# From step 1 on SyncE issues every copy within the chip, and the plan is re-timed for it

## The chip, the cores and the metric

The kernel runs on 1 core of one Trainium2 chip. The metric is the device time of one execution in microseconds (us). Where a per cent is given it is of the time before, 480.99 us.

## The reference

For 4 batches and 8 heads a gated linear attention runs over 768 tokens; its output is the input of a two-layer block with a piecewise gate:

```python
f = 1.0 / (1.0 + np.exp(-f_logit))
for t in range(S):                       # S = 768, D = 48
    state = f[:, :, t, :, None] * state + np.einsum('bhd,bhe->bhde', k[:, :, t], v[:, :, t])
    y[:, :, t] = np.einsum('bhd,bhde->bhe', q[:, :, t], state)
...
h = x @ w_in                             # x: 3072 x 384, w_in: 384 x 2048
g = np.where(h >= 1, h, np.where(h <= -1, 0.0, (h + 1) ** 2 / 4.0))
return g @ w_out                         # w_out: 2048 x 384
```

## The kernel before

**Steps and units.** The 768 tokens are cut into 6 steps of 128 tokens. Each step has 4 pairs of heads (the numbers n = 0 to 23 in the tables are 4 times the step plus the pair). Its attention result fills three tiles x (one row of tile per feature, 512 columns: 4 batches of 128 tokens), and on these the two-layer block runs in 16 units, one for each 128 of the 2048 middle features, so 96 units in all, numbered u = 0 to 95. `unit_1(u)` is nine matmuls of 128x512 into a bank `ph` (line 259); ScalarE (lines 262, 265), VectorE (270), ScalarE (273, giving `ghi`) and VectorE (276, giving `glo`) then make the two parts of the gate; `unit_2(u)` is nine matmuls from these into the three banks `po` (line 283). TensorE runs unit_1(u), then unit_2(u-1): between a unit's two halves lie the second half of the unit before it and the first half of the one after. Around step 1's end two units are cut in halves and paired differently; that is not touched here.

**Groups.** The attention of later steps is strewn between the units as groups of small matmuls. For a pair of numbers n, n+1 there are four kinds: the transposes of keys (`TURNS`: on TensorE for step 1, as stream transposes, line 735, on VectorE from step 2), the scores (line 702, then masks on line 708), the state parts (line 850, sums on lines 854 and 863; `begin` with them, line 757), and the outputs (line 789 and 757), after which lines 740 and 741 round the result into x. `VISITS` names for each n the unit after whose first half the scores, the state parts and the outputs stand.

**Copies within the chip.** The fourth pair of heads has no tile of its own in the block: its rows (16 of them at a time) are put into the spare rows of the other tiles. Hence two kinds of copies by DMA, both issued by `move` on line 301: `kq<-kq` gathers keys and queries of the fourth pair (6 pieces per step, line 584), and `x<-y` spreads its result over the three x tiles (6 pieces per step or half step, line 814). The six x pieces have to land before unit_1 of the next step's first unit. Every second piece goes by ScalarE's queue, the others by SyncE's. All other transfers (line 296: f, kq and v of the steps, raw weights, results) are issued by SyncE.

**Order.** A planner (`Plan.order`) lists the operations by engine: it walks through time with a cost for each operation (table `COST`, ns) and takes on each engine the operation that is due first. TensorE's own order is that of the program text. An engine executes its list in order, so an instruction that waits holds up whatever stands behind it; this holds for the DMA issues in ScalarE's list too. The DMAs share 8 semaphores in turn (`DMAHW0` to `DMAHW7` in the built program): an issue waits until the transfer that used its semaphore 8 transfers earlier has landed. Where the plan has a gap on TensorE in the first 20 us it puts matmuls on zeros there (line 337).

**Weights.** The weights come as 8-byte floats, 512 KB a piece into three buffers `raw` (25 pieces, used in the first 80 us); ScalarE (line 390), VectorE (392), ScalarE (396: the high part) and VectorE (397: the low part) split each. Later all pieces are loaded once more and searched for values out of range (line 407).

Of the kernel before, what the change touches and what calls it, by code (L numbers as in the profile page):

```python
# [10 lines left out]
F32 = mybir.dt.float32  # L11
# [14 lines left out]
NP = H // 2  # L26
# [15 lines left out]
NT = 3  # L42

SLICE = (1, 2, 0)
# [6 lines left out]

HOP, LANDING, PER_KB, NEAR, ADDING = 200, 2000, 3.0, 3500, 1500
LATENCY = dict(PE=235, ACT=140, DVE=110, POOL=150)
COST = dict(mm=227, narrow=120, scores=1100, scores_half=550, heads=950, thirds=1110, both=1090, begin=480, before=930, part=560, states=850, parts=830, turn=350, first=110, last=95,
            rows=316, turned_rows=150, scan=1140, dve=602, small=200, sums=467, gate=600, act=575, bits=660, round=485, copy=520, turned=412, sig=538, decay=226,
            issue=480, near=600, least=300)


TURNS = {4: 5, 5: 6, 6: 10, 7: 10, 8: 16, 9: 16, 10: 24, 11: 24, 12: 31, 13: 31, 14: 37, 15: 37, 16: 44, 17: 44, 18: 53, 19: 53, 20: 61, 21: 61, 22: 70, 23: 70}
VISITS = {4: (6, 7, 8), 6: (10, 11, 13), 8: (18, 22, 24), 10: (24, 28, 29), 12: (31, 35, 37), 14: (37, 43, 44), 16: (44, 48, 53), 18: (53, 57, 61), 20: (61, 67, 70), 22: (70, 72, 77)}  # L60
START = (("scores", 0), ("mask", 0, 0), ("mask", 0, 1), ("last", 0), ("scores", 1), ("mask", 1, 0), ("mask", 1, 1), ("last", 1),
         ("scores", 2, 0), ("last", 2, 0), ("scores", 2, 1), ("last", 2, 1), ("first", 0), ("first", 1),
         ("mask", 2, 1), ("mask", 3, 1), ("mask", 2, 0), ("mask", 3, 0), ("second", 0), ("second", 1), ("second", 2), ("second", 3))
# [17 lines left out]
class Plan:  # L81
# [7 lines left out]
    def add(self, engine, cost, emit, *deps, kb=0, near=0):  # L89
# [9 lines left out]
        spread(list(deps))  # L99
        cost, kind = COST[cost] if isinstance(cost, str) else cost, cost  # L100
        if engine == "PE":
# [67 lines left out]
def gla_moe(ctx: ExitStack, tc: tile.TileContext, ff, kqd, f0, vv, vad, vbd, wd, fixedd, gates, values, headsd, out):  # L169
    nc = tc.nc  # L170
# [12 lines left out]
    kq = tiles(NP, [128, 2 * N + B], F32, "kq")  # L183
# [12 lines left out]
    y3 = const.tile([R, 2, N], F32R, name="y3")  # L196
# [25 lines left out]
    def whole(t):  # L222
        return t[:, 2 * N:]
# [73 lines left out]

    def move(k, dst, src, *deps, near=NEAR):

        e, q = (("SP", nc.sync), ("ACT", nc.scalar))[k % 2]  # L300
        return add(e, "near", lambda: q.dma_start(dst, src), *deps, near=near)

    def vec(cost, fn, *deps):
# [15 lines left out]
    set_kq = add("POOL", 1500, lambda: nc.gpsimd.memset(kq[NP - 1], 0.0))  # L319
# [110 lines left out]
    turn = {"n": 0}  # L430
# [11 lines left out]
    state_of, moved, x_of, unit_in, unit_out = {}, {}, {}, {}, {}  # L442
# [106 lines left out]
    def elementwise(n):  # L549

        i, p = pairs[n]
        c = att[n] = {}
        k = n // 2 % 2
        by_half = i == HALVES
        h = p // 2 if by_half else None
        mine = ((0, 1), (2, 3))[p % 2] if by_half else (p,)
        ours = range(NT * i, NT * i + NT) if p == NP - 1 and not by_half else [NT * i + q for q in mine if q < NT]
        for m in ours:
            if by_half:
                gate(m, (h,))  # L560
            elif gates_of[m] is None:
                gate(m)
        before = [old(j, "y", "st") for j in (range(n - 2 * NP + NP - p, n - p) if i == HALVES + 1 else (n - 4,))]
        if by_half:
            k = p % 2
            if h == 0:
                c["lv"] = dma(v[k], vv[i, k], 384, before, att[2]["st"])
            else:
                c["lv"] = att[n - 2]["lv"]
        elif n % 2:  # L570
            c["lv"] = att[n - 1]["lv"]
        elif i == 0:
            c["lv"] = dma(va if p == 0 else vb, vad if p == 0 else vbd, 512 if p == 0 else 768)
        else:
            c["lv"] = dma(v[k], vv[i, p // 2], 384, before, att[2]["st"], moved[HALVES, 1])
        if NP - 1 in mine:

            every = range(NT * i, NT * i + NT)
            cols = slice(HW * h, HW * h + HW) if by_half else slice(0, 2 * N + B) if i else slice(0, N)
            gone = [old(NP * i - j, "sc", "y", "tr", "db") for j in ((1, 2, 3, 4) if i == HALVES + 1 else (1,))]  # L580
            for t, m in enumerate(every):
                o = gates_of[m]
                d = [o[a][h] for a in ("km", "qm", "pf")] if by_half else [o["km"], o["qm"], o["pf"][0]] if i else o["km"]
                to = [move(k, kq[NP - 1][z + 16 * SLICE[t]:z + 16 * SLICE[t] + 16, cols], kq[t][r:r + 16, cols], d, set_kq, gone, near=NEAR) for k, (r, z) in enumerate(((48, 0), (112, 64)))]
                o["to"] = o.get("to", []) + to
                c.setdefault("to", []).extend(to)
        if by_half:
            c["kq"] = [[gates_of[NT * i + q][a][h] for a in ("km", "qm")] for q in mine if q < NT] + c.get("to", [])
        else:
            c["kq"] = c["to"] if p == NP - 1 else [gates_of[m][a] for m in ours for a in ("km", "qm")]  # L590
        c["db"] = []
        for e, q in enumerate(mine if i > 0 else ()):
            nb = B // len(mine)
            at = n % 2 * B * D + e * nb * D
            bs = slice(0, B) if h is None else slice(h * nb, h * nb + nb)
            pf = whole(kq[q]) if h is None else kq[q][:, HW * h + 2 * HN:HW * (h + 1)]
            d = c["to"] if q == NP - 1 else gates_of[NT * i + q]["pf"][0 if h is None else h]

            def decayed(at=at, q=q, bs=bs, pf=pf):
                for j, b in enumerate(range(bs.start, bs.stop)):  # L600
                    nc.scalar.activation(ds[:, at + j * D:at + (j + 1) * D], state[:, q * B + b], AF.Copy, scale=pf[:R, j:j + 1])  # L601

            c["db"].append(sca(nb * COST["decay"], decayed, d, state_of[i - 1, q // 2], old(n - 2, "y", "se"), set_ds))
# [171 lines left out]
    def outputs(n):  # L775

        i, p = pairs[n]
        c, d = att[n], att[n + 1]
        held, where = c["to_y"]
        half_of = p // 2 if i == HALVES else None  # L780

        def emit():
            for k, before in ((1, later), (0, ds)):
                for m in range(B):
                    for e, h in TILES:
                        g, at = where[m][e]
                        (r, z), (pr, b) = HEADS[h], blocks(g)[at]
                        a = (g % 2 * B + at) * D
                        nc.tensor.matmul(held[h][1][64 * e:64 * e + D, m, T * k:T * k + T], before[r:z, a:a + D], query(g, pr, b)[r:z, T * k:T * k + T],  # L789
                                         start=False, stop=False)  # L790

        c["ys"] = add("PE", "before", emit, c["db"], d["db"], c["later"], c["yb"])
        y = c["y"] = d["y"] = add("PE", "part", attended(n, False), c["ys"])
        xt = x[i % 2]
        free = unit_in.get((i - 2, NJ - 1))

        def third(t):
            return [moved.get((i - 1, k)) for k in (None, 0, 1)] + c["se"] if t == NT else [free]

        if half_of is None:  # L800
            for t, (b, ps, _) in zip((p, p + 1), held):
                hi, lo = (y3[:, 0], y3[:, 1]) if t == NT else (xt[:, t, 0], xt[:, t, 1])
                x_of[i, t] = rounded(b, wide(ps)[:R], hi[:R], lo[:R], y, third(t))
            cs = ALL
        else:
            cs = cols_of(half_of)
            (b0, ps, _), (b1, qs, _) = held
            x_of[i, 0] = x_of[i, 2] = rounded(b0, wide(ps)[:R].rearrange("r (t n) -> r t n", t=2), xt[:R, 0:3:2, 0, cs], xt[:R, 0:3:2, 1, cs], y, third(0))
            x_of[i, 1] = rounded(b1, wide(qs)[:R, 0:HN], xt[:R, 1, 0, cs], xt[:R, 1, 1, cs], y, third(1), 300)
            x_of[i, NT] = rounded(b1, wide(qs)[:R, HN:], y3[:, 0, cs], y3[:, 1, cs], y, third(NT), 300)  # L810
            banks[b1] = x_of[i, 1] + x_of[i, NT]
        if p > 0 or half_of is not None:

            moved[i, half_of] = [move(k, xt[r:r + 16, t, :, cs].bitcast(F32), y3[z + 16 * SLICE[t]:z + 16 * SLICE[t] + 16, :, cs].bitcast(F32), x_of[i, NT], x_of[i, t])
                                 for t in range(NT) for k, (r, z) in enumerate(((48, 0), (112, 64)))]

    def states(n):

# [225 lines left out]
    def of_second(t):  # L1044
# [5 lines left out]
        else:  # L1050
            y = thirds(t, a, [deps, att[2]["lv"], att[0]["am"], att[1]["am"]])
            if t == 2:
# [5 lines left out]
                turn=lambda n: transpose_tensor(n, {0: 1, 1: 5}.get(n)), states=lambda n: states(n))  # L1058
# [7 lines left out]

    for n, u in TURNS.items():
        groups.setdefault(u, []).append((1, n))
# [44 lines left out]
    with tc.If(bad > 0):  # L1113
        for c in range(2 * NW):
            split_again(c)
        heads = const.tile([R, 2], F32, name="heads")
# [4 lines left out]
        with tc.For_i(0, S, 1) as t:  # L1121
            e, z, y = tmp
            vb, fkq, z = e[:R, 0:768], e[:R, 768:816], z[:R, 0:768]
# [130 lines left out]
```

## Time and profile before

| what | value |
|---|---|
| time, median of 3 runs (lowest to highest) | 480.99 us (480.82 to 481.69) |
| the profiled execution's own time | 479.54 us |
| span of its profile | 477.8 us |
| TensorE (PE) busy | 466.0 us, 98% of the span |
| VectorE (DVE), ScalarE (ACT) busy | 367.0 us (77%), 264.4 us (55%) |
| granted TensorE clock, mean | 0.996 |

A row of a chain of waits gives start, length and what ran or was waited for. In a timeline a row gives start, length, engine, line, operation, result and operands, a count, and in brackets the idle time before it with what ended it. ACTq and SPq are the queues of ScalarE and SyncE: their rows are DMA issues. The names are those of the program without buffer numbers, so `raw<-in_w` is any weight piece.

### The profile page before, as it was taken

What the parts mean: (1) busy time and instruction counts of PE and PEld (TensorE: products, weight loads), DVE (VectorE), ACT (ScalarE), POOL (GpSimd) and SP (SyncE); (2) the same over time, 40 slices, a digit from 0 to 9 for tenths busy, and PEclk for the clock granted to TensorE, in tenths of its full rate; (3) what the DMA queues carried; (4) which work ended last, traced back from release to release, by engine and by line L of the source; (5) the groups of instructions that cost most, each with busy time, mean ns of one, the idle gap of its engine ahead of it and who ended that gap; (6) DMA issues with size and microseconds to landing.
All of it is one profiled execution on the core that took longest, in us unless ns stands there. A gap on an engine that the chain in (4) does not pass through costs nothing.

```text
span 477.8 us, 11262 instructions
## 1 busy us (share of the span) xinstructions
PE 466.0 (98%) x4659; PEld 383.7 (80%) x4659; DVE 367.0 (77%) x720; ACT 264.4 (55%) x488; POOL 26.5 (6%) x77
## 2 busy tenths in 40 slices
PE   9999999999999999999999999998999999999994
PEld 4877888889988788888888888886888888888883
DVE  7998997949999999999799988775576555655332
ACT  4679989746446474455455465354436454544451
POOL 4111100000010200002000001000000000000000
PEclk9999999999999999999999999999999999999998
DMA  8788665074013052132143053034411234431002
GB/s 297 239 309 289 233 212 183 2 254 139 1 35 124 23 155 109 36 123 72 63 133 102 1 168 100 10 120 126 144 44 47 88 91 121 155 88 45 2 0 72
DMA packets 21722, 54.42 MB, mean 114 GB/s; under 512 B 3328, under 2 KB 6656, under 8 KB 21664
## 3 DMA queue, kind: packets, MB, share of 16 engines
q1 hardware_dynamic: 20320, 51.56, 33.0%
q10 hardware_dynamic: 1344, 2.07, 1.9%
q8 instruction: 38, 0.62, 0.5%
q14 instruction: 20, 0.16, 0.1%
HBM read 44.76 MB, written 4.72 MB: 104 GB/s over the span
## 4 chain that ended last, share of the span: by engine, by line
PE 87%; DMA 4%; DVE 3%; ACT 3%; issue 0%; ACTq 0%
PE po L283 40%; PE ph L259 38%; DMA raw<-in_w 3%; PE pa L757 2%; PE pa L789 2%; DMA f<-in_f 2%; PE ph L702 1%; PE pa L850 1%; ACT bits L390 1%; DVE w L502 1%; PE ph L850 1%; DVE x L741 1%; DVE f L509 0%; ACT f L498 0%; DVE bits L392 0%; ACT act L265 0%
## 5 line engine op out<-in xcount | busy, mean ns | idle before, releaser
L259 PE MATMUL ph<-x,w_hi 128*128 128x512 f32 (+1 forms) x606 | 146.3, 377 | 0.0
L262 ACT ACTIVATE act<-ph,half 128x512 f32<-128x512 f32 x96 | 66.0, 688 | 118.3 <-PE ph L259 108.5
L259 PEld LDWEIGHTS ph<-x,w_hi 128*128 128x128 f32 x606 | 109.7, 188 | 20.8
L270 DVE SCALAR_TENSOR_TENSOR act<-ph,act 128x512 f32<-128x512 f32 x96 | 65.9, 687 | 64.3 <-ACT act L265 63.9
L273 ACT CAST ghi<-act 128x512 fp32r<-128x512 f32 x96 | 59.7, 622 | 60.6 <-DVE act L270 60.5
L283 PE MATMUL po<-ghi,w_hi 128*128 128x512 f32 (+1 forms) x305 | 86.4, 389 | 3.1 <-ACT ghi L273 3.1
L283 PE MATMUL po<-ghi,w_lo 128*128 128x512 f32 (+1 forms) x305 | 83.1, 378 | 0.0
L283 PE MATMUL po<-glo,w_hi 128*128 128x512 f32 (+1 forms) x305 | 82.8, 377 | 0.0
L259 PE MATMUL ph<-x,w_lo 128*128 128x512 f32 (+1 forms) x303 | 81.3, 376 | 0.0
L276 DVE TENSOR_TENSOR glo<-act,ghi 128x512 fp32r<-128x512 f32 x96 | 66.0, 687 | 17.4 <-ACT ghi L273 15.9
L735 DVE STREAM_TRANSPOSE kn<-kq 32x128 f32<-32x128 f32 x224 | 67.8, 303 | 3.6
L283 PEld LDWEIGHTS po<-ghi,w_hi 128*128 128x128 f32 x305 | 53.0, 188 | 14.3 <-ACT ghi L273 4.2
L283 PEld LDWEIGHTS po<-ghi,w_lo 128*128 128x128 f32 x305 | 55.3, 188 | 10.9
L283 PEld LDWEIGHTS po<-glo,w_hi 128*128 128x128 f32 x305 | 55.2, 188 | 10.9 <-DVE glo L276 0.2
L265 ACT ACTIVATE act<-act 128x512 f32<-128x512 f32 x96 | 60.8, 633 | 5.5 <-DMA raw<-in_w 2.0
L259 PEld LDWEIGHTS ph<-x,w_lo 128*128 128x128 f32 x303 | 55.3, 188 | 10.4
L407 DVE TENSOR_REDUCE ok<-raw 128x1 f32<-128x512 f32 x48 | 31.3, 675 | 5.5 <-DMA raw<-in_w 5.3
L506 POOL COPY end<-w 128x4 f32<-128x4 f32 (+1 forms) x23 | 9.4, 409 | 258.1 <-DVE w L502 257.9
L502 DVE TENSOR_TENSOR_SCAN w<-f,least_w 128x512 f32<-128x512 f32 (+1 forms) x21 | 21.1, 1011 | 1.9 <-ACT f L498 1.8
L390 ACT ACTIVATE bits<-raw,top_of 128x512 uint32<-128x512 fp8e4 (+1 forms) x25 | 18.6, 748 | 5.6 <-DMA raw<-in_w 5.2
L509 DVE TENSOR_TENSOR_SCAN f<-f,rec 128x512 f32<-128x512 f32 (+1 forms) x21 | 21.2, 1011 | 0.0
L601 ACT ACTIVATE sd<-sd,kq 112x48 f32<-112x48 f32 x80 | 19.9, 330 | 0.0
(122 smaller groups left out, 384.9 us busy)
## 6 DMA issues: line engine op xcount, KB each, us to landing
raw<-in_w SPq DMA_DIRECT2D x24, 512.0 KB, 3.6
raw<-in_w SPq DMA_DIRECT2D x21, 511.6 KB, 4.3
kq<-in_kq SPq DMA_DIRECT2D x18, 512.0 KB, 5.0
out_y<-raw SPq DMA_DIRECT2D x17, 256.0 KB, 2.1
v<-in_v SPq DMA_DIRECT2D x10, 384.0 KB, 5.5
f<-in_f SPq DMA_DIRECT2D x13, 256.5 KB, 3.0
raw<-in_w SPq DMA_DIRECT2D x4, 382.9 KB, 7.5
f<-in_f SPq DMA_DIRECT2D x7, 128.5 KB, 4.2
```

The source lines that it names most:

```text
L259: nc.tensor.matmul(ps[:, to], w_in(w_hi if high else w_lo, j, kt), xt[:, kt, t, c], start=(n == 0), stop=(n == 8))
L262: nc.scalar.activation(a, ps, AF.Relu, bias=half, scale=0.5)
L265: nc.scalar.activation(a, a, AF.Square)
L270: nc.vector.scalar_tensor_tensor(out=a, in0=ps, scalar=1.0, in1=a, op0=ALU.max, op1=ALU.min)
L273: nc.scalar.copy(hi, a)
L276: nc.vector.tensor_tensor(out=lo, in0=a, in1=hi.bitcast(F32), op=ALU.subtract)
L283: nc.tensor.matmul(po[e][:, c], w_out(part, j, e), g[:, of], start=(j == 0 and n == 0 and c.start == 0), stop=(j == NJ - 1 and n == 2))
L390: m = sca(COST["bits"] * n // W, lambda: nc.scalar.activation(t, top, AF.Abs, bias=top_of, scale=2.0 ** 30), loaded, made[k - 4] if k >= 4 ...
L407: seen.append(vec("dve", lambda z=z, op=op: nc.vector.tensor_reduce(out=ok[:, 1 + NG + z + c:2 + NG + z + c], in_=words_of(raw[2])[1].bitc ...
L502: s1 = vec(COST["scan"] if count == 1 else 602, lambda bwd=bwd, u0=u0, u1=u1: nc.vector.tensor_tensor_scan(out=wide(w[:, u0:u1]), data0=bw ...
L509: s2 = vec(COST["scan"] if count == 1 else 602, lambda fwd=fwd, b0=b0, b1=b1: nc.vector.tensor_tensor_scan(out=fwd, data0=fwd, data1=wide( ...
L735: nc.vector.transpose(kn[n % 2][u:u + 32, ::-1, r:r + 32], src[:, :, u:u + 32])
```

## The change

In `move`'s two places the piece number no longer picks the queue, except for step 0's `kq<-kq`. The planner's costs of step 0's score groups are lowered, so that the plan holds TensorE busy for a shorter time in the first 25 us, and most entries of the two tables move by one to three units. The planner then lists every engine's operations anew. The diff, with the tables cut to two entries each:

```diff
-COST = dict(..., scores=1100, scores_half=550, heads=950, thirds=1110, ...)
+COST = dict(..., scores=1000, scores_half=500, heads=960, thirds=1020, ...)
...
-TURNS = {..., 8: 16, 9: 16, 10: 24, 11: 24, ...}
+TURNS = {..., 8: 17, 9: 17, 10: 25, 11: 25, ...}
-VISITS = {..., 8: (18, 22, 24), ..., 14: (37, 43, 44), ..., 18: (53, 57, 61), ...}
+VISITS = {..., 8: (19, 24, 25), ..., 14: (37, 43, 45), ..., 18: (53, 57, 60), ...}
...
     def move(k, dst, src, *deps, near=NEAR):
-        e, q = (("SP", nc.sync), ("ACT", nc.scalar))[k % 2]
+        e, q = (("SP", nc.sync), ("ACT", nc.scalar))[k]
         return add(e, "near", lambda: q.dma_start(dst, src), *deps, near=near)
...
-                to = [move(k, kq[NP - 1][...], kq[t][r:r + 16, cols], d, set_kq, gone, near=NEAR) for k, (r, z) in enumerate(((48, 0), (112, 64)))]
+                to = [move(0 if i else k, kq[NP - 1][...], kq[t][r:r + 16, cols], d, set_kq, gone, near=NEAR) for k, (r, z) in enumerate(((48, 0), (112, 64)))]
...
-            moved[i, half_of] = [move(k, xt[...], y3[...], x_of[i, NT], x_of[i, t])
-                                 for t in range(NT) for k, (r, z) in enumerate(((48, 0), (112, 64)))]
+            moved[i, half_of] = [move(0, xt[...], y3[...], x_of[i, NT], x_of[i, t])
+                                 for t in range(NT) for r, z in ((48, 0), (112, 64))]
```

The order of the lists changes on every engine. Three places follow as the built programs have them. First ScalarE behind the outputs of n = 18, the group that ends step 4's attention (`x_85` and `y_87` are its rounded results, `act` and `ghi` the gates of the units). Before:

```order
L740 CAST x_85<-pa_108 112x512
L740 CAST y_87<-pa_109 112x512
L273 CAST ghi_89<-act_84 128x512
L601 ACTIVATE sd<-sd,kq_68 112x48 x4
L601 ACTIVATE sd<-sd,kq_69 112x48 x4
L301 DMA kq_71<-kq_68 16x1028
L301 DMA x_85<-y_87 16x1024 x3
L262 ACTIVATE act_83<-ph_111,half 128x512
L301 DMA kq_71<-kq_69 16x1028
L265 ACTIVATE act_83<-act_83 128x512
L301 DMA kq_71<-kq_70 16x1028
L273 CAST ghi_88<-act_83 128x512
```

The same place now, one unit earlier in the program:

```order
L740 CAST x_85<-pa_108 112x512
L740 CAST y_87<-pa_109 112x512
L601 ACTIVATE sd<-sd,kq_68 112x48 x4
L273 CAST ghi_88<-act_83 128x512
L601 ACTIVATE sd<-sd,kq_69 112x48 x4
L262 ACTIVATE act_84<-ph_112,half 128x512
L265 ACTIVATE act_84<-act_84 128x512
L273 CAST ghi_89<-act_84 128x512
```

Six DMA issues that stood between the steps of two units' gates are gone from ScalarE's list.

Second, ScalarE in the first weights of units 4 to 7, from the gate of unit 2 (`act_0_83`) to that of unit 3 (`ghi_1_89`); `raw_0`, `raw_1`, `raw_2` are the three weight buffers. Before:

```order
L390 ACTIVATE bits_3_98<-raw_1_93,top_of_107 128x512
L262 ACTIVATE act_0_83<-ph0_111,half_104 128x512
L724 COPY kn_0_80<-pa1_109 128x4x112
L265 ACTIVATE act_0_83<-act_0_83 128x512
L724 COPY kn_1_81<-pa2_110 128x4x112
L390 ACTIVATE bits_0_95<-raw_2_94,top_of_107 128x512
L396 CAST w_hi_99<-bits_3_98 128x512
L273 CAST ghi_0_88<-act_0_83 128x512
L390 ACTIVATE bits_1_96<-raw_0_92,top_of_107 128x512
```

Now:

```order
L262 ACTIVATE act_0_83<-ph0_111,half_104 128x512
L724 COPY kn_0_80<-pa1_109 128x4x112
L265 ACTIVATE act_0_83<-act_0_83 128x512
L724 COPY kn_1_81<-pa2_110 128x4x112
L390 ACTIVATE bits_3_98<-raw_1_93,top_of_107 128x512
L390 ACTIVATE bits_1_96<-raw_0_92,top_of_107 128x512
L273 CAST ghi_0_88<-act_0_83 128x512
L396 CAST w_hi_99<-bits_3_98 128x512
L390 ACTIVATE bits_0_95<-raw_2_94,top_of_107 128x512
```

Unit 2's gate and two copies now stand ahead of the first of these weight pieces, and the piece in `raw_0` ahead of that in `raw_2`; SyncE's list has these two loads exchanged as well.

Third, SyncE where step 3's result goes over into x (`x_86<-y_87`), behind the outputs of n = 14. Before:

```order
L296 DMA kq_70<-in_kq 128x1024
L301 DMA kq_71<-kq_68 16x1028
L301 DMA kq_71<-kq_69 16x1028
L296 DMA v<-in_v 128x768
L301 DMA x_86<-y_87 16x1024 x3
L301 DMA kq_71<-kq_70 16x1028
```

Now:

```order
L296 DMA kq_70<-in_kq 128x1024
L301 DMA kq_71<-kq_68 16x1028 x2
L301 DMA kq_71<-kq_69 16x1028 x2
L296 DMA v<-in_v 128x768
L301 DMA x_86<-y_87 16x1024 x6
L301 DMA kq_71<-kq_70 16x1028 x2
```

The order is the same; SyncE issues the twofold number of copies.

More of the change, by code (lines that the diff above doesn't have):

```diff
@@ L53 @@
 LATENCY = dict(PE=235, ACT=140, DVE=110, POOL=150)
-COST = dict(mm=227, narrow=120, scores=1100, scores_half=550, heads=950, thirds=1110, both=1090, begin=480, before=930, part=560, states=850, parts=830, turn=350, first=110, last=95,
+COST = dict(mm=227, narrow=120, scores=1000, scores_half=500, heads=960, thirds=1020, both=1090, begin=480, before=930, part=560, states=850, parts=830, turn=350, first=110, last=95,
             rows=316, turned_rows=150, scan=1140, dve=602, small=200, sums=467, gate=600, act=575, bits=660, round=485, copy=520, turned=412, sig=538, decay=226,
             issue=480, near=600, least=300)
-TURNS = {4: 5, 5: 6, 6: 10, 7: 10, 8: 16, 9: 16, 10: 24, 11: 24, 12: 31, 13: 31, 14: 37, 15: 37, 16: 44, 17: 44, 18: 53, 19: 53, 20: 61, 21: 61, 22: 70, 23: 70}
-VISITS = {4: (6, 7, 8), 6: (10, 11, 13), 8: (18, 22, 24), 10: (24, 28, 29), 12: (31, 35, 37), 14: (37, 43, 44), 16: (44, 48, 53), 18: (53, 57, 61), 20: (61, 67, 70), 22: (70, 72, 77)}
+TURNS = {4: 5, 5: 6, 6: 10, 7: 10, 8: 17, 9: 17, 10: 25, 11: 25, 12: 29, 13: 29, 14: 37, 15: 37, 16: 45, 17: 45, 18: 53, 19: 53, 20: 60, 21: 60, 22: 69, 23: 69}
+VISITS = {4: (6, 7, 9), 6: (10, 12, 13), 8: (19, 24, 25), 10: (25, 28, 29), 12: (32, 35, 37), 14: (37, 43, 45), 16: (45, 48, 53), 18: (53, 57, 60), 20: (60, 65, 69), 22: (69, 73, 74)}
 START = (("scores", 0), ("mask", 0, 0), ("mask", 0, 1), ("last", 0), ("scores", 1), ("mask", 1, 0), ("mask", 1, 1), ("last", 1),
@@ L583, in elementwise @@
                 d = [o[a][h] for a in ("km", "qm", "pf")] if by_half else [o["km"], o["qm"], o["pf"][0]] if i else o["km"]
-                to = [move(k, kq[NP - 1][z + 16 * SLICE[t]:z + 16 * SLICE[t] + 16, cols], kq[t][r:r + 16, cols], d, set_kq, gone, near=NEAR) for k, (r, z) in enumerate(((48, 0), (112, 64)))]
+                to = [move(0 if i else k, kq[NP - 1][z + 16 * SLICE[t]:z + 16 * SLICE[t] + 16, cols], kq[t][r:r + 16, cols], d, set_kq, gone, near=NEAR) for k, (r, z) in enumerate(((48, 0), (112, 64)))]
                 o["to"] = o.get("to", []) + to
@@ L812, in outputs @@
         if p > 0 or half_of is not None:
-            moved[i, half_of] = [move(k, xt[r:r + 16, t, :, cs].bitcast(F32), y3[z + 16 * SLICE[t]:z + 16 * SLICE[t] + 16, :, cs].bitcast(F32), x_of[i, NT], x_of[i, t])
-                                 for t in range(NT) for k, (r, z) in enumerate(((48, 0), (112, 64)))]
+            moved[i, half_of] = [move(0, xt[r:r + 16, t, :, cs].bitcast(F32), y3[z + 16 * SLICE[t]:z + 16 * SLICE[t] + 16, :, cs].bitcast(F32), x_of[i, NT], x_of[i, t])
+                                 for t in range(NT) for r, z in ((48, 0), (112, 64))]
     def states(n):
```

## The prediction

> **What bounds the kernel now.** I read busy time by stretches of the span first, since an average over the span would hide which stage has room. Columns: stretch in us, its length, then busy us (instructions) of PE, PEld, DVE, ACT and POOL, granted clock, DMA share, GB/s.
>
> ```profile
> 20.00:46.00 26.00, 24.66 (x205) 19.30 (x206) 23.29 (x45) 21.77 (x43) 2.06 (x9) 1.00 0.82 271
> 46.00:300.00 254.00, 254.00 (x3036) 213.77 (x3035) 229.10 (x470) 151.56 (x291) 16.88 (x45) 1.00 0.34 110
> 300.00:330.00 30.00, 27.70 (x271) 22.68 (x270) 19.50 (x39) 13.70 (x27) 0.00 (x0) 1.00 0.29 85
> 330.00:470.90 140.90, 140.90 (x977) 116.17 (x975) 77.47 (x132) 68.03 (x112) 0.00 (x0) 1.00 0.23 73
> ```
>
> From 46 to 300 us and from 330 to 470.9 TensorE has no idle time at all, at full granted clock. In these 395 us nothing that another engine does faster can shorten the kernel; it can only be made longer, by a new wait. Room is left in two places: 2.3 us between 300 and 330, and 1.34 us between 20 and 46. The next view names what TensorE waited for (engine, line, waited for, total us, times, longest).
>
> ```profile
> PE po L283 <- ACT ghi L273: 3.1, 4, 2.3
> ...
> PE ph L654 <- ACT kn L648: 0.3, 1, 0.3
> ```
>
> The one large wait is for a gate. The chain of waits and the timelines of PE and ACT show where.
>
> ```profile
> 319.12 6.39 DMA raw<-in_w
> ...
> 325.53 0.51 ACTq L301
> ...
> 326.09 0.64 ACT act L265
> ```
> ```profile
> 320.93 0.84 PE L259 MATMUL ph<-x,w_lo 128*128 128x512 f32 x3
> 325.01 0.84 PE L259 MATMUL ph<-x,w_lo 128*128 128x512 f32 x3
> 328.15 0.98 PE L283 MATMUL po<-ghi,w_hi 128*128 128x512 f32 x3 [2.30 <-ACT ghi L273]
> ```
> ```profile
> 320.05 3.34 ACTq L301 DMA_DIRECT2D x<-y  x3
> 323.44 0.69 ACT L262 ACTIVATE act<-ph,half 128x512 f32<-128x512 f32 x1 [3.47 <-DMA v<-in_v]
> 325.53 0.51 ACTq L301 DMA_DIRECT2D kq<-kq  x1
> 326.09 0.63 ACT L265 ACTIVATE act<-act 128x512 f32<-128x512 f32 x1 [1.96 <-DMA raw<-in_w]
> ...
> 327.48 0.62 ACT L273 CAST ghi<-act 128x512 fp32r<-128x512 f32 x1 [0.76 <-DVE act L270]
> ```
>
> The unit's first half was done at 321.77 (320.93 + 0.84). ScalarE could have begun its gate (L262) there, but a copy x<-y stood ahead of it in its list until 323.39, and that issue waited for v's load; then a copy kq<-kq held L265 until a weight load had landed. Neither copy needs v or the weight: each waits for the semaphore that it shares with them. From L265's start to the end of `ghi` are 2.01 us (326.09 to 328.10), L262 takes 0.69: undisturbed `ghi` is ready at 321.77 + 0.69 + 2.01 = 324.5. TensorE is through with the next unit's first half at about 325.7 (three matmuls from 325.01). So the gate had 1.2 us to spare, came 3.6 late, and cost 2.4 (2.30 in the row, where modelled ends overlap; 2.46 between the starts of the matmuls on either side, beyond their usual distance. I take 2.46).
>
> **The change part by part.** *The queue.* This row group counts what is issued (columns: instructions, their length min/median/max in ns, first and last start).
>
> ```profile
> L301 ACTq DMA_DIRECT2D kq<-kq x21: 514/517/712, 6.8 to 326.2; - x21
> L301 SPq DMA_DIRECT2D x<-y x18: 507/586/1062, 70.6 to 396.0; - x18
> L301 ACTq DMA_DIRECT2D x<-y x18: 514/604/954, 70.6 to 396.3; - x18
> DMA to landing us min/median/max: 1.9/3.5/6.2
> ```
>
> Of ScalarE's 39 copies the 3 of step 0 stay; 18 + 18 = 36 move, about 20 us of issue time (18 x 0.517 + 18 x 0.604) taken out of ScalarE's list. Most of it lies beside a saturated TensorE and is worth nothing. The one place where it isn't is the stall at 325: both instructions that held the gate leave ScalarE's list there (first of the three orders above), so all **2.46 us** go. What is late next at that spot is nothing within 1.2 us, by the sum above. ScalarE can't be held by any other unit's copies either, since none are left behind step 0's.
>
> SyncE issues them instead. Nothing computes on SyncE, but what stands behind the added copies starts later: about 0.55 us a copy, and any wait of a copy for its shared semaphore. The x copies have a due time. The tightest joint is step 3's result, outputs of n = 14, wanted by unit 48:
>
> ```profile
> 240.92 0.68 DVE L741 TENSOR_TENSOR y<-pa,y 112x512 fp32r<-112x512 f32 x1
> ```
> ```profile
> 237.24 1.04 PE pa L789 x64
> ...
> 239.66 2.27 PE po L283 x9
> ...
> 250.10 2.04 PE ph L259 x9
> ```
>
> y is ready at 241.6 and the row at 250.10 is unit 47's first half, unit 48's follows two rows of 2.04 later. The outputs now stand one unit nearer to it (45 for 44), so in these rows' times unit 48 takes the place at 250.10: 8.5 us behind y. Before SyncE's x copies now stand four kq<-kq instead of two, 1.0 us more, so the first goes at 242.6, the sixth five issues of 0.586 later at 245.6. With the median landing of 3.5 it is there at 249.1, 1.0 to spare; with the longest of 6.2 at 251.8, 1.7 late. The pieces there took 3.5 and 3.8, as the next rows show (KB each, median us to landing), so I take **0** and keep 1.7 for the rivals.
>
> ```profile
> x<-y SPq DMA_DIRECT2D x3, 64.0 KB, 3.5
> x<-y ACTq DMA_DIRECT2D x3, 64.0 KB, 3.8
> ```
>
> Here a rule weighs against the change. First the rows, from the joint at 319 to 323.5:
>
> ```profile
> raw<-in_w SPq DMA_DIRECT2D x1, 512.0 KB, 6.4
> x<-y SPq DMA_DIRECT2D x3, 64.0 KB, 5.0
> x<-y ACTq DMA_DIRECT2D x3, 64.0 KB, 5.7
> ```
>
> ScalarE's small pieces took 5.7 us beside a 512 KB load of SyncE's, SyncE's own 5.0: the second queue let nothing overtake. The Trainium skill ("DMA: Bandwidth & Descriptors", Queues, rings and completion order) says that a DMA engine takes turns, packet by packet, between the queue rows that have work; by it a piece on ScalarE's row could pass a big load on SyncE's, and in one row all would stand behind the load. By that rule the moved pieces would land up to the load's own time later; the two rows above don't bear it out.
>
> *The head.* Between 24 and 46 us ScalarE is the bound; the chain there reads:
>
> ```profile
> 29.92 6.36 DMA raw<-in_w
> ...
> 36.31 0.76 ACT bits L390
> 37.07 0.58 ACT act L262
> ...
> 39.02 0.66 ACT bits L390
> ...
> 44.53 0.52 ACTq L301
> 45.05 0.30 ACT ghi L273
> ```
>
> The list is rearranged (second of the three orders): unit 2's gate and two copies, 1.95 us in this chain (37.07 to 39.02), now stand ahead of the wait for the weight piece that lands at 36.28 (29.92 + 6.36), so they fill the wait for it. But the next L390 now takes the piece in raw_0, which came third, and its load is issued later, at 33.37 in this trace. With a landing time of 4.3 us, the median of this kind of load, it is there at 37.7, and with the 6.36 of the row above at 39.7. The L390 ahead of it ends at 37.1 (36.31 + 0.76): a new wait of 0.6 to 2.6 comes in. One kq<-kq issue (0.52) leaves the chain before unit 3's `ghi`, one f L498 (0.30) joins it. The sum for `ghi`: before, 9.04 us from 36.31 to its end at 45.35; less 1.95, less 0.52, plus 0.30 is 6.87, and I add 0.5 for work that stood beside the kq<-kq issue and now follows in line. 36.31 + 7.4 = 43.7, plus 0.6 to 2.6 is 44.3 to 46.3: between -1.1 and +1.0. A gain can't pass TensorE's idle time there, 1.34 by the first row of all. The load meets the same crowd as the one of 6.36, though, so I take less than half of the better end, **-0.4**.
>
> *The plan.* The 25 places where groups of attention stand stay 25, with the same matmuls in each, moved by one to three units: **0** for TensorE as long as what they wait for is there. Two more matmuls on zeros (line 337) enter the first 20 us, under the wait for L648 (0.3 of it is left in the row of waits) and others for ScalarE: **0**, and at the most two times 0.23. DVE is the engine to look at:
>
> ```profile
> 140.00:180.00 40.00, 40.00 (x562) 32.91 (x561) 38.50 (x86) 22.87 (x48) 3.25 (x6) 1.00 0.29 90
> ```
> ```profile
> L735 DVE STREAM_TRANSPOSE kn<-kq 32x128 f32<-32x128 f32 x224 | 67.8, 303 | 3.6
> L276 DVE TENSOR_TENSOR glo<-act,ghi 128x512 fp32r<-128x512 f32 x96 | 66.0, 687 | 17.4 <-ACT ghi L273 15.9
> ```
>
> It has 1.5 us of 40 left. The state parts of n = 8 now stand at unit 24 (22 before), those of n = 10 stay at 28: 4 units apart instead of 6. In DVE's list stand between them 32 transposes (9.7 us), seven gate operations like L276 (4.8), and seven masks, roundings, sums and scalings that I put at the same size or less (4 to 4.8): 18.5 to 19.3 us. TensorE takes there 4 units of 4.1 (8 of the 2.04 above) and one group with outputs of about 2.4 (237.24 to 239.66): 18.7. The transposes, which TensorE needs first, stand ahead of most of the rest. So it is level, with no wait over about 0.6: **0**, and a rival.
>
> The sum: 479.54 - 2.46 - 0.4 = **476.7** for the profiled execution. That one lies 1.45 below the median of 480.99; I carry the difference over, and forecast 480.99 - 2.86 = **478.1**.
>
> **The rivals.** About 0.2%, 0.96 us, is what a measurement here can tell from no change: faster means below 480.03, slower above 481.95.
>
> *More in the head.* If the piece in raw_0 lands early, all of the head's 1.34 us go: 480.99 - 2.46 - 1.34 = 477.2. For it: ScalarE is the bound of that chain. Against: DMA is 82% busy there. Chance 0.10.
>
> *SyncE's added issues make a load for ScalarE late.* ScalarE's L498 waits for f; if one such wait grows by the 2.5 us that the longest took (row below) ahead of a gate with 1.2 to spare, TensorE stands for 1.3: 478.1 + 1.3 = 479.4. Chance 0.12.
>
> ```profile
> ACT f L498 <- DMA f<-in_f: 5.0, 4, 2.5
> ```
>
> *The pieces of x are late in their one queue.* At unit 48 and at unit 32 (outputs now three units ahead in both) unit_1 waits for the last piece, up to 1.7 at each: 478.1 + 3.4 = 481.5, no change to be told. For it: 6.2 occurs. Against: 3.5 to 3.8 at that joint. By the skill's rule above this would be the likely way; as the trace speaks against it, 0.10.
>
> *DVE becomes the bound, the slower side.* If DVE comes to unit 24 already behind, `glo` and the transposes for `begin` at 28 are late by as much, since it has no spare in those four units, and TensorE waits for it. It turns slower when these waits pass 3.85 us (481.95 - 478.1); the seven gate operations and the seven small ones all ahead of the last transposes, with half of them again from the unit before, would make 5, giving 478.1 + 5 = 483.1. For it: the 38.50 of 40 above, and the two units less. Against: the sum is level, and TensorE didn't wait for DVE once from 46 to 300 us. Chance 0.08.
>
> **How the numbers follow.** The forecast, 478.1, has 0.60. The range reaches from 476.8 (the bigger head gain, less 0.4 for the scatter of the runs, whose lowest and highest lie 0.9 apart) to 481.0, which holds the forecast with its head term from -1.1 to +1.0, the late load, and late pieces at one joint (478.1 + 1.7 = 479.8); outside are late pieces at both and the slower case. Faster: 0.60 + 0.10 + 0.12 = 0.82, less 0.02 for the late load with the worst of the head (479.4 + 1.4), 0.80; same: 0.10 + 0.02 = 0.12; slower 0.08.
>
> **What would show it right or wrong.** Right: no PE wait for `ghi` over 1 us after 300, no ACTq row on L301 behind the first 50 us, PE busy in every microsecond from 46 to its last group, the span shorter by some 2.9. The head term is wrong if PE's idle time from 20 to 46 is not near 1.34 - 0.4 = 0.9. Wrong in the whole: a PE wait for DMA x<-y at the first unit_1 of a step, a wait of `begin`'s matmuls for kn, or an ACT wait for f that a PE wait for `ghi` follows.

## The result and the profile after

| | before | changed | ratio (95% interval) |
|---|---|---|---|
| median, 6 runs each (lowest to highest) | 482.16 us (480.82 to 483.75) | 476.90 us (475.89 to 477.82) | 0.989 (0.986 to 0.992) |
| profiled execution: time, span | 479.54, 477.8 | 476.89, 475.1 | |

The changed kernel is faster by 5.3 us in the medians, and by 2.7 us between the two profiled executions. That these two differ by a factor of two is the main question below.

The stretches of the changed kernel, in the columns of the prediction (the last one ends near TensorE's last matmul):

```profile
20.00:46.00 26.00, 25.43 (x213) 20.27 (x210) 24.87 (x49) 23.50 (x49) 3.38 (x12) 1.00 0.87 282
46.00:300.00 254.00, 253.78 (x3033) 213.19 (x3032) 227.84 (x467) 149.62 (x287) 15.86 (x42) 1.00 0.35 108
300.00:330.00 30.00, 30.00 (x282) 24.93 (x281) 19.92 (x39) 14.80 (x29) 0.00 (x0) 1.00 0.34 93
330.00:468.10 138.10, 137.98 (x964) 113.73 (x962) 76.49 (x130) 67.11 (x112) 0.00 (x0) 1.00 0.24 72
```

TensorE's idle time is 0.57 us in the head (1.34 before), 0.22 in the long middle (0 before), and 0 from 300 to 330 us (2.30 before). What TensorE waits for now:

```profile
PE ph L337 <- DVE zeros L309: 1.0, 1, 1.0
PE ph L938 <- DVE x L741: 0.3, 1, 0.3
PE po L283 <- ACT ghi L273: 0.3, 1, 0.3
PE ph L259 <- DVE y L854: 0.2, 1, 0.2
```

The gate's 3.1 us are down to 0.3. The wait for y (L854) is new, 0.2 us. ScalarE's timeline at the joint of n = 18, which before held three copies x<-y and three kq<-kq:

```profile
313.10 1.02 ACT L601 ACTIVATE sd<-sd,kq 112x48 f32<-112x48 f32 x4
314.02 0.61 ACT L273 CAST ghi<-act 128x512 fp32r<-128x512 f32 x1
314.53 1.01 ACT L601 ACTIVATE sd<-sd,kq 112x48 f32<-112x48 f32 x4
317.38 0.69 ACT L262 ACTIVATE act<-ph,half 128x512 f32<-128x512 f32 x1 [1.84 <-PE ph L259]
318.10 0.63 ACT L265 ACTIVATE act<-act 128x512 f32<-128x512 f32 x1
319.49 0.62 ACT L273 CAST ghi<-act 128x512 fp32r<-128x512 f32 x1 [0.76 <-DVE act L270]
```

L262 now waits for nothing but TensorE's first half, and the steps of the gate follow one another as in any other unit. The copies' issues are all SyncE's (columns as before), but for step 0's three:

```profile
L301 SPq DMA_DIRECT2D kq<-kq x39: 507/541/1231, 11.5 to 320.6; - x39
L301 SPq DMA_DIRECT2D x<-y x36: 507/588/1472, 72.8 to 382.7; - x36
L301 ACTq DMA_DIRECT2D kq<-kq x3: 513/514/600, 6.7 to 15.5; - x3
DMA to landing us min/median/max: 1.9/2.9/7.3
```

The median landing of a copy fell from 3.5 to 2.9 us. The joint that the prediction reckoned to be the tightest, from the issues of the transfers (KB each, median us to landing) and from TensorE's first matmuls of unit 48:

```profile
x<-y SPq DMA_DIRECT2D x6, 64.0 KB, 2.4
```
```profile
253.71 1.52 PE L259 MATMUL ph<-x,w_hi 128*128 128x512 f32 x6
```

The sixth copy was issued at 249.4 and landed at 251.65 in the trace, 2.3 us later; unit 48 begins at 253.71. The copy is there 2.1 us ahead.

### The profile page after: what moved, and what is told of

The parts are those of the page before. It is cut to its first block, busy times and chain, and to the rows that moved or that the text cites. A ratio compares the mean times of both kernels' runs of the same rounds, so it can differ in the third digit from the quotient of the medians.

```text
span 475.1 us, 11247 instructions
## 1 busy us (share of the span) xinstructions
PE 466.2 (98%) x4661; PEld 383.9 (81%) x4661; DVE 366.5 (77%) x720; ACT 263.7 (56%) x488; POOL 26.5 (6%) x77
## 4 chain that ended last, share of the span: by engine, by line
PE 80%; DVE 7%; DMA 6%; ACT 4%; issue 1%; SPq 1%; DVEq 0%
PE po L283 37%; PE ph L259 36%; DMA raw<-in_w 4%; PE pa L789 2%; PE pa L757 2%; DVE bits L392 2%; DVE w_lo L397 1%; PE ph L702 1%; ACT bits L390 1%; DMA kq<-in_kq 1%; DVE act L270 1%; DVE glo L276 1%; DVE w L502 1%; PE pa L850 1%; DVE f L509 1%
## 5 line engine op out<-in xcount | busy, mean ns | idle before, releaser
L262 ACT ACTIVATE act<-ph,half 128x512 f32<-128x512 f32 x96 | 66.0, 687 | 117.2 <-PE ph L259 117.2
L270 DVE SCALAR_TENSOR_TENSOR act<-ph,act 128x512 f32<-128x512 f32 x96 | 65.9, 687 | 64.8 <-ACT act L265 63.9
L273 ACT CAST ghi<-act 128x512 fp32r<-128x512 f32 x96 | 59.6, 620 | 60.6 <-DVE act L270 60.6
L265 ACT ACTIVATE act<-act 128x512 f32<-128x512 f32 x96 | 60.8, 633 | 2.7
L407 DVE TENSOR_REDUCE ok<-raw 128x1 f32<-128x512 f32 x48 | 31.1, 674 | 1.6 <-DMA raw<-in_w 1.4
L601 ACT ACTIVATE sd<-sd,kq 112x48 f32<-112x48 f32 x80 | 20.3, 330 | 0.1
```

What stands on the lines that cost most here:

```text
L262: nc.scalar.activation(a, ps, AF.Relu, bias=half, scale=0.5)
L265: nc.scalar.activation(a, a, AF.Square)
L270: nc.vector.scalar_tensor_tensor(out=a, in0=ps, scalar=1.0, in1=a, op0=ALU.max, op1=ALU.min)
L273: nc.scalar.copy(hi, a)
L407: seen.append(vec("dve", lambda z=z, op=op: nc.vector.tensor_reduce(out=ok[:, 1 + NG + z + c:2 + NG + z + c], in_=words_of(raw[2])[1].bitc ...
```

## The experiments

Each kernel stands beside runs of the kernel before on the same chip. The first four, the next four and the last four ran together; within a group medians may be compared, across groups the ratios.

| kernel | median us | before beside it | ratio (95% interval) |
|---|---|---|---|
| again | 481.58 | 481.08 | 1.000 (0.998 to 1.003) |
| queue_only | 478.16 | 481.08 | 0.993 (0.990 to 0.996) |
| plan_only | 479.28 | 481.08 | 0.996 (0.993 to 0.998) |
| one_step | 477.30 | 481.08 | 0.993 (0.991 to 0.996) |
| after_again | 476.14 | 481.22 | 0.990 (0.987 to 0.993) |
| one_step_b | 477.37 | 481.22 | 0.993 (0.991 to 0.995) |
| plan_one | 478.38 | 481.22 | 0.995 (0.993 to 0.997) |
| one_back | 478.04 | 481.22 | 0.994 (0.991 to 0.996) |
| queue_again | 478.02 | 481.05 | 0.993 (0.991 to 0.996) |
| cost_queue | 477.82 | 481.05 | 0.992 (0.989 to 0.994) |
| late_out | 480.62 | 481.05 | 1.000 (0.998 to 1.002) |
| late_two | 482.86 | 481.05 | 1.002 (1.000 to 1.004) |

**again: the kernel before, a second look.** No edit.

> The kernel before, unchanged, as a second look at its profile. Theory (one stall behind the outputs of n = 18, the same in every execution): ratio within 0.2% of 1; TensorE again waits 2 to 3 us for ghi near 325 us, and ScalarE's copies on line 301 stand ahead of that gate. Rival (the kernel's executions lose time in other places as well, which the one profile did not show, since the measured gain of 5.3 us is twice the 2.7 us by which the two profiles differ): this profile's span is 479 to 481 us, and TensorE has a second wait behind a copy of ScalarE's of 1 us or more at another step's joint (near 170, 245 or 385 us) or in the head.

The time is the same. Its profile has a span of 479.2 us, 1.4 more than the first. Its stretch from 300 to 330 us, ScalarE there, and TensorE behind the gate:

```profile
300.00:330.00 30.00, 26.82 (x267) 21.99 (x266) 19.11 (x38) 13.41 (x28) 0.00 (x0) 1.00 0.29 76
```
```profile
323.20 0.69 ACT L262 ACTIVATE act<-ph,half 128x512 f32<-128x512 f32 x1 [2.98 <-DMA v<-in_v]
326.65 0.51 ACTq L301 DMA_DIRECT2D kq<-kq  x1
327.21 0.63 ACT L265 ACTIVATE act<-act 128x512 f32<-128x512 f32 x1 [3.33 <-DMA raw<-in_w]
```
```profile
329.27 0.96 PE L283 MATMUL po<-ghi,w_hi 128*128 128x512 f32 x3 [3.18 <-ACT ghi L273]
```

The same stall at the same place, from the same copies, but 3.2 us (2.3 in the first profile): here the weight load held L265 for 3.33 us instead of 1.96. The head's stalls near 40 and 45 us, together 0.8 us in the first profile, are not there. A second large wait behind a copy is not there either, against the rival; the largest waits for a gate besides behind 46 us are of 0.2 us, at 120 and 178. So the place is the same in both profiles, and its price varies with the landing of a load.

**one_step, one_step_b: one joint's copies alone.** The same kernel, on two occasions.

```diff
-to = [move(k, kq[NP - 1]...
+to = [move(0 if i == 5 else k, kq[NP - 1]...
-moved[i, half_of] = [move(k, xt...
+moved[i, half_of] = [move(0 if i == 4 else k, xt...
```

> The kernel before with only two sets of copies moved to SyncE: those of step 4's result into x, and the kq copies for step 5 that stand beside them. TensorE's order and everything ahead of 300 us stay as they were. Theory (the one stall at 325): 2.3 to 2.6 us less than before (ratio 0.9945 to 0.9955), TensorE without idle time from 300 to 330 us. Rival (another wait follows when that one goes, the load or DVE): under 1 us less (0.998 or above). If before loses at several joints, this too gains 2.5 but less than the kernel with all copies moved.

> The kernel before with only the copies of one joint moved to SyncE (step 4's result into x, kq for step 5), a second time, beside the changed kernel. Theory: 3 us less than before (0.992 to 0.995), and the same as the changed kernel within 0.2%. Rival (the plan gains by itself): 1 to 2 us above the changed kernel.

In medians 3.8 us less than before, both times; TensorE's order and all engines' lists up to the joint are those of before. The stretch of one_step from 300 to 330 us, and what is late next: TensorE, DVE and SyncE behind it:

```profile
300.00:330.00 30.00, 30.00 (x282) 24.93 (x281) 18.70 (x37) 15.04 (x29) 0.00 (x0) 1.00 0.28 76
```
```profile
337.76 0.97 PE L283 MATMUL po<-ghi,w_hi 128*128 128x512 f32 x3 [0.24 <-ACT ghi L273]
```
```profile
335.17 1.28 DVE L407 TENSOR_REDUCE ok<-raw 128x1 f32<-128x512 f32 x2 [1.64 <-DMA raw<-in_w]
336.37 0.68 DVE L270 SCALAR_TENSOR_TENSOR act<-ph,act 128x512 f32<-128x512 f32 x1
```
```profile
324.64 1.15 SPq L301 DMA_DIRECT2D kq<-kq x2
325.83 5.48 SPq L296 DMA_DIRECT2D raw<-in_w  x2
```

The stall is gone whole: ScalarE's copies at this one joint caused it. A small one comes in its place, 0.24 us in the row (0.40 by the distance of the matmuls' starts; 0.36 in one_step_b): DVE's list has the search of a weight piece (L407) ahead of the gate's L270, and that piece's load is the second of the two that stand on SyncE behind the copies. It starts when DVE has searched the piece of the first (330.98 in the trace) and lands at 335.15. So what stands behind the copies on SyncE feeds an engine that works on gates. That the copies made these loads late is read from the order of SyncE's list; no run tests it alone.

**one_back: that joint's copies put back.** The changed kernel with ScalarE issuing every second copy at this joint again; TensorE's order stays.

```diff
-to = [move(0 if i else k, kq[NP - 1]...
+to = [move(k if i in (0, 5) else 0, kq[NP - 1]...
-moved[i, half_of] = [move(0, xt...
+moved[i, half_of] = [move(k if i == 4 else 0, xt...
```

> The changed kernel with every second one of that one joint's copies back on ScalarE (step 4's result into x, kq for step 5); TensorE's order is that of the changed kernel. Theory (what stalls is a gate behind a copy whose issue waits for a transfer that used its semaphore 8 transfers before): a TensorE wait for ghi of 0.5 to 3 us comes back between 315 and 330 us, of a size that depends on which transfer that is, and it is the time lost. Rival (the copies' own issue time of 0.5 us each holds the gates): under 0.3 us lost, since a gate there has 1.2 us to spare. Rival (the new plan has the outputs one unit earlier and so avoids the stall by itself): no wait, no time lost.

1.9 us slower than after_again beside it, 1.5 by the spans (476.6 and 475.1). ScalarE and TensorE at the joint:

```profile
319.29 0.51 ACTq L301 DMA_DIRECT2D kq<-kq  x1
319.85 0.69 ACT L262 ACTIVATE act<-ph,half 128x512 f32<-128x512 f32 x1 [4.10 <-DMA x<-y]
```
```profile
322.89 0.96 PE L283 MATMUL po<-ghi,w_hi 128*128 128x512 f32 x3 [1.26 <-ACT ghi L273]
```

One copy, issued at 319.29, held the gate. In the trace its semaphore is the one that v's load had used eight transfers before; ScalarE waits for that semaphore ahead of the copy, and the load landed at 319.21. So the stall comes back with the copies, as the theory had it, and its size is set by what used the semaphore before. 0.5 us an issue would have fitted into the 1.2 us to spare; the wait doesn't. The new plan's earlier outputs don't avoid it by themselves.

**plan_only, plan_one: the new tables with ScalarE's copies.** The first has the new tables and costs and the old choice of the queue; the second adds one_step's two edits.

> The new tables and costs, with every second copy on ScalarE as before. Theory: the head's gain of about 1 us stays, a stall behind a copy of ScalarE's stays at one of the joints: 0.5 to 1.5 us less than before (0.997 to 0.999). Rival (the copies alone): the same as before within 0.2%, or above it if a copy of ScalarE's meets a big load at more joints in the new plan. Second rival (the plan makes most of the gain): 3 us less or more (0.994 or below).

> The new tables and costs, and of the copies only those of step 4's result into x and of kq for step 5 on SyncE. Theory (only that joint's copies count): as the changed kernel within 0.2%, TensorE without a wait for ghi from 300 to 330 us. Rival (ScalarE's copies cost at other joints too, as the 0.57 us near 177 us with the new plan and ScalarE's copies hints): 0.5 to 1.5 us more than the changed kernel.

plan_only gains 1.8 us: the stall is there, now at 323 us, but smaller (0.83 us by the starts of the matmuls), and another of 0.57 us at 178. plan_one has none there, yet lies 2.2 us above the changed kernel: not only that joint counts in the new plan. ScalarE and TensorE of plan_one at the joint of n = 10:

```profile
176.32 1.16 ACTq L301 DMA_DIRECT2D kq<-kq  x2
177.52 0.62 ACT L273 CAST ghi<-act 128x512 fp32r<-128x512 f32 x1 [2.46 <-DMA x<-y]
```
```profile
178.19 0.96 PE L283 MATMUL po<-ghi,w_hi 128*128 128x512 f32 x3 [0.44 <-ACT ghi L273]
```

Two copies kq<-kq ahead of L273 wait for an earlier x<-y, and the gate is late by 0.4 to 0.6 us, which the changed kernel's profiles don't show. The spans of the two profiles differ by 1.6 us (476.7 and 475.1). Most of the rest of that lies in the head, where plan_one waits 1.1 us for x (L741) and 0.7 for kn (L648), the changed kernel 0.3 and 0.4 for x and not for kn; what of that is scatter these runs don't tell.

**after_again: the changed kernel, a second look.**

> The changed kernel, unchanged, on one chip with the next three. Its first comparison with before stood at 0.989 (0.986 to 0.992), its first profile was 2.7 us shorter than the first profile of before. In the kernel before, the stall near 325 us was 2.5 us in one profile and 3.3 in the other, and the stalls of 0.9 us in the head near 40 and 45 us were in one profile and not in the other. Theory (the stall is the gain, its size differs from execution to execution; the plan adds little): ratio 0.990 to 0.994, within 0.2% of the kernel that moves only one joint's copies. Rival (the new plan gains 1 to 2 us by itself): ratio 0.987 to 0.990, and below that kernel by 1 us or more.

0.990, and a span of 475.1 as at first, with stalls at the same few places. Of the two ways expected, the medians lean to the rival: 1.2 us below one_step_b on the same chip. The intervals overlap, and the spans of the two profiles differ by 0.1 us (475.1 and 475.2), although one_step_b's holds the small wait at 337 us that the new tables' profiles don't have.

**queue_only, queue_again: the copies on SyncE, tables and costs of before.** The same kernel twice.

> All copies on SyncE from step 1 on, with the tables and costs of before. Theory (the queue takes away 2.5 us late, the new plan gains about 1 us in the head): 2.5 to 3 us less than before (ratio 0.994 to 0.995), no TensorE wait for ghi over 1 us behind 300 us, the head as before within 0.6 us. Rival (before loses in several joints, all by ScalarE's copies): 4 to 5.5 us less (0.989 to 0.992). Second rival (the plan makes most of the gain): at most 1.5 us less (0.997 or above).

> All copies on SyncE with the tables and costs of before, a second time. Its first profile had a TensorE wait of 1.85 us near 48.8 us, ahead of which a weight load took 7.1 us to land. Theory (scatter of the loads in the head): that wait is under 0.5 us or gone in this profile, and the time is that of the kernel which moves only one joint's copies, 0.992 to 0.994. Rival (the old list puts a gate behind that load in every execution, and the new costs cure it): a wait over 1 us for ghi again between 43 and 50 us, and the kernel with the new costs and the old tables 1 us faster than this one.

2.9 and 3.0 us less than before, no more than one joint's copies bring. The stall at 325 us is gone, and another has come, in both profiles. TensorE near 50 us in queue_only and in queue_again, then the chain of queue_again to it:

```profile
50.70 0.98 PE L283 MATMUL po<-ghi,w_hi 128*128 128x512 f32 x3 [1.69 <-ACT ghi L273]
```
```profile
50.51 0.97 PE L283 MATMUL po<-ghi,w_hi 128*128 128x512 f32 x3 [1.11 <-ACT ghi L273]
```
```profile
39.46 5.78 DMA raw<-in_w
45.24 0.02 issue
45.26 0.77 ACT bits L390
46.03 0.51 ACT w_hi L396
46.54 0.46 ACT sd L601 x2
47.01 0.57 ACT act L262
47.58 0.64 ACT bits L390
48.22 0.52 ACT act L265
48.74 0.90 ACT sd L601 x4
49.64 0.31 ACT f L498
49.95 0.52 ACT ghi L273
```

ScalarE waits for a weight piece ahead of a gate, and then six L601 and an L498 stand ahead of and between the gate's steps, 1.7 us. I had taken the first one for scatter of the loads; since it recurs behind the same instructions, I put it down to the list that the planner makes with the new queues and the old costs. TensorE's wait for y (L854) is longer too, 0.5 and 0.8 us against 0.2 in the changed kernel.

**cost_queue: the copies on SyncE and the new costs, the tables of before.** It is queue_only with the changed kernel's `COST`.

> All copies on SyncE, step 0's scores and the other costs as in the changed kernel, but the tables TURNS and VISITS of before. Theory (moving the groups between units is worth nothing, the changed list of the head is worth about 1 us at most): 476 to 477 us, ratio 0.989 to 0.992, the same as the changed kernel within 0.2%. Rival (the tables make the rest of the gain): as the kernel with the queue alone, 0.992 to 0.994, 1 us or more above the changed kernel.

0.992, between the two that were expected, and its interval holds both. By the medians it does not differ from queue_again beside it (477.82 and 478.02), so the 1 us that queue_again's rival expected is not shown. Its profile has no wait for a gate over 0.2 us between 45 and 300 us and none for y: there the new costs, which rearrange the head, remove what the queue alone brings in. Waits of 0.8 us each for kn (L648) and for x (L741) stand in its head. The small wait behind L407 is there again (0.42 us in the row at 338.3); the tables are the old ones.

**late_out, late_two: how near the x copies are to their due time.** The changed kernel with the outputs of n = 14 one unit later, and no matmuls on zeros put into gaps behind 200 us; in late_two ScalarE issues every second copy at that joint.

```diff
-VISITS = {..., 14: (37, 43, 45), ...}
+VISITS = {..., 14: (37, 43, 46), ...}
-                    warm(int(gap * 0.9 / 230))
+                    warm(int(gap * 0.9 / 230) if o.start < 200000 else 0)
```

> The changed kernel with the outputs of n = 14 one unit later (46 instead of 45) and no matmuls on zeros behind the first stretch: it tests the due time of the x copies. In the two profiles of the changed kernel the last of the six landed 2.1 us ahead of unit 48's first matmul. One unit is 4.1 us, so by the sum TensorE waits 1.5 to 2.5 us for the last x copy at unit 48, and the kernel is 1.5 to 3 us slower than the changed kernel. Rival (SyncE's list, not the time of y, sets when the copies go): a wait under 0.5 us.

> As the kernel before it, but at that joint (step 3's result into x, kq for step 4) every second copy is issued by ScalarE again. What one queue costs there is the difference between the two waits at unit 48. If issues set the landing (three x copies and one or two kq copies fewer on SyncE, some 0.6 us each, 2.4 to 3 us): no wait at unit 48, or under 0.5 us. If the transfers set it: the same wait as with one queue within 0.5 us.

late_out has a span of 478.8 us, 3.7 above the changed kernel's. Its first matmul of unit 48, and the copies ahead of it:

```profile
256.53 1.16 PE L259 MATMUL ph<-x,w_hi 128*128 128x512 f32 x4 [0.79 <-DMA x<-y]
```
```profile
x<-y SPq DMA_DIRECT2D x6, 64.0 KB, 2.3
```

The wait for the copies exists, 0.8 us, half of what was expected: the planner put v's load behind the copies here, and each landed 2.3 us after its issue. The load of f went behind them as well, and ScalarE waited for it ahead of a gate:

```profile
261.50 0.64 ACT L498 ACTIVATE f<-f 128x513 f32<-128x513 f32 x1 [2.38 <-DMA f<-in_f]
```

TensorE's waits near 264 us, behind that gate and the copies of results that follow it, come to 1.4 in all. This is the way that the prediction's rival of a load late for ScalarE described, at nearly its price (1.3). Of the rest of the 3.7 us, 0.8 is idle time of TensorE ahead of 46 us (2.3 against 1.6), which differs between profiles. The margin of the joint is thus under one unit: moved by 4.1 us it is spent.

late_two didn't test what it was meant to, because v's load stands ahead of the copies again, but it shows the first mechanism once more, at a joint where neither kernel had it:

```profile
251.45 3.39 ACTq L301 DMA_DIRECT2D x<-y  x3
254.87 0.62 ACT L273 CAST ghi<-act 128x512 fp32r<-128x512 f32 x1 [4.29 <-DMA x<-y]
```
```profile
255.54 0.98 PE L283 MATMUL po<-ghi,w_hi 128*128 128x512 f32 x3 [1.78 <-ACT ghi L273]
```

ScalarE is idle for 4.29 us ahead of `ghi`, behind three copies. The first waited for y until 251.4, the second until 253.7 for the kq copy that had used its semaphore (it landed at 253.66 in the trace). TensorE waits 1.8, and the kernel is 2.2 us slower than late_out beside it. The last of SyncE's x copies landed at 257.76, 1.4 us later than late_out's last (256.40). Here the second queue did not bring x sooner and cost a gate.

## Why the prediction was right, and where it was off

*What bounds the kernel, and the queue's term.* Right, and shown both ways: one joint's copies taken off ScalarE remove the stall whole (one_step), put back they bring it back (one_back), and at another joint they make one (late_two).

*The size.* The forecast was -2.86, the medians moved by -5.3 and -5.1 (ratio 0.989 and 0.990). The median of 476.90 lies 0.1 us above the lower end of the range (476.8), so the range held it narrowly. For the profiled execution the sum, 476.7, was right to 0.2. The step that was off is the one that carried the 1.45 us between the profiled execution and the median over unchanged. The profiled execution of before was one of the quicker ones, 479.54 where the 28 runs of the second group had a median of 481.22 and reached from 478.12 to 483.27; the changed kernel's own profile stood at its median (476.89 and 476.90).

Two things can make those other executions longer, and no run parts them. One is the stall itself: it is the time by which a load's landing overran, and it took 2.46 us in one profile and 3.34 in the other (by the starts of the matmuls). The other is the granted clock. Its mean is 0.996 and 0.995 in the two profiles of the kernel before. Of 90 executions of that kernel in the three groups (the longest, 486.03 us, left out), 31 have 0.995 or more and a median of 480.06 us; the other 59 have 0.989 to 0.994 and a median of 481.60. That is 1.5 us more, about what was carried over. The changed kernel has 0.995 or more in all of its 12. So has every other kernel here in all executions, but for the three that keep a stall of 0.8 us or more behind ScalarE's copies: plan_only (1 of 12 below), one_back (1 of 12) and late_two (3 of 10). Beside the executions of before at 0.995 or more on the same chip (medians 480.36 and 479.62), one_step and one_step_b gain 3.1 and 2.3 us instead of 3.8, near the stall's size in the two profiles, and after_again 3.5 instead of 5.1.

A lower clock thus seems to come with the stall. But choosing executions by their clock may also choose them by their stall, and none of the profiles is of an execution with the lower clock. So why it is lower, and what share of the 1.5 us it makes, stays open.

*What is late next.* The prediction said nothing within 1.2 us at that spot. It looked at the gate of the next unit, and on SyncE at the x copies and f. What it left out is the weight search on DVE, which waits for a load behind the copies: 0.4 to 0.6 us by the starts of the matmuls in four of the five profiles with the old tables and this joint's copies on SyncE (queue_only's has none). No profile of the new tables has it, and that is luck as far as the prediction goes, since it did not look there.

*The x copies.* 1.0 us to spare was forecast, 2.1 measured: the last copy landed 2.3 us after its issue, not 3.5. The rival of late copies didn't come; late_out shows that it was under one unit away. The rows of the prediction spoke against the rule of the Trainium skill ("DMA: Bandwidth & Descriptors", Queues, rings and completion order) by which a second queue row could pass a big load. In late_two one of ScalarE's copies did, issued at 251.45 and landed at 256.18 beside v's load, 251.19 to 256.76; the next, issued at 253.68, landed behind the load at 257.58, and the third one's landing is not on record. A gain of 0.6 us for one piece is in the sense of that rule; it is less than the 1.8 us that the copies cost on ScalarE there, and in one queue the median copy landed earlier (2.9 us against 3.5), not later.

*The head.* -0.4 was forecast, the profiles give 0.77 less idle time from 20 to 46 us. But the kernel before, run again, has 0.83 idle there (25.17 busy of 26) instead of 1.34, and the changed kernel, run again, 0.93 instead of 0.57:

```profile
20.00:46.00 26.00, 25.07 (x208) 19.89 (x205) 24.81 (x49) 23.18 (x48) 3.30 (x12) 1.00 0.87 286
```

So no gain of the head above the scatter is shown. The use of the new list seems to be another one than forecast: with the queue alone two profiles have a wait of 1.1 to 1.7 us near 50 us, and with the new costs no profile has it (late_two's has one of 1.0 us at 46), though the medians of queue_again and cost_queue don't differ. The prediction treated the head as a term of its own; by these profiles it is a cover for a wait that the first term brings.

*The plan.* Zero was taken. Between the profiles of one_step_b and after_again that holds to 0.1 us. Whether the tables bring more of the 1.2 us by which after_again lies below one_step_b stays open: cost_queue and the changed kernel overlap in their intervals.

*DVE as the bound* didn't come: no wait for a transpose of step 2, and the new wait for y is 0.2 us. That one is still against the sign that TensorE would be busy in every microsecond from 46 on.

## What to carry to other kernels

A DMA issue in the list of an engine that computes is a wait with a hidden length: ask which earlier transfer its semaphore belonged to, not only what its data depend on, and put such issues on an engine whose list holds nothing else. When issues move to another queue, follow the transfers behind them to the engines that read them, down to work as unimportant as a test, since it stands in a list with gates. A stall that ends with a landing has a spread, so take its size from more than one profile, set the forecast from the median of runs, and compare the granted clock of the runs that were not profiled with that of the one that was.

## What was not expected of the hardware

The same 64 KB copy landed 2.3 us after its issue with no load issued just ahead of it (late_out, six copies; the last load had gone 2.7 us before the first of them), and 4.2 to 4.3 in the median (late_two, both queues) with a 384 KB load just ahead, which itself took 5.6:

```profile
v<-in_v SPq DMA_DIRECT2D x1, 384.0 KB, 5.6
x<-y ACTq DMA_DIRECT2D x3, 64.0 KB, 4.3
x<-y SPq DMA_DIRECT2D x3, 64.0 KB, 4.2
```

What stands ahead of a small copy counted for 2 us in the medians, which queue it was in for 0.1, with two landings of ScalarE's three on record. And the executions of one program differ more than the change in the plan is worth: those of the kernel before had 5.2 us between the lowest and the highest of 28 (the second group), those of the changed kernel 1.9 and 2.6 us between six.
